# Attention units with partitions in (segment, head pair) order, and the last chunk stored in transfers of 32 rows from two queues

## The chip, the core and the metric

One core of a Trainium2 chip runs the whole program. The metric is the device time of one execution in microseconds; lower is better. Five engines work side by side, each through its own list of instructions in order: TensorE (PE in the profile, its weight loads PEld), VectorE (DVE), ScalarE (ACT), GpSimd (POOL) and SyncE (SP), which only issues transfers. Sixteen DMA engines carry the transfers between HBM and the on-chip memory (SBUF). Matmul results stand in PSUM.

## The reference

`q`, `k`, `v` have shape (8 batches, 8 heads, 576 tokens, 64). For each head two attentions are added, and a two-layer network follows:

```python
q_d, k_d, v_d = (x.reshape(B, H, 144, 4, D).mean(axis=3) for x in (q, k, v))
out_up = np.repeat(sm_attn(q_d, k_d, v_d), 4, axis=2)
mask = np.abs(pos[:, None] - pos[None, :]) < 4
scores = np.where(mask, scale * np.matmul(q, k.transpose(0, 1, 3, 2)), -1e9)
out = out_up + softmax(scores) @ v
x = out.transpose(0, 2, 1, 3).reshape(4608, 512)
h = x @ w_in                                      # 512 -> 2048
y = (np.maximum(h, 0) + alpha * np.minimum(h, 0)) @ w_out   # 2048 -> 512
```

The first attention runs over averages of four tokens; the second sees, for each token, the seven tokens at a distance below four. All inputs and outputs are float32.

## The kernel before

**The network.** The 4608 token rows are cut into 18 chunks of 256 rows (`T`). A chunk takes eight steps (`NP`), so there are 144 steps (`NS`). A step's `hidden` (L752) makes two blocks of 128 hidden columns in 24 matmuls. ACT and DVE apply the slope (L760 to L764), ACT and POOL split the result in a high and a low part `gh` and `gl` (L769, L69), and `product` (L796) adds its 12 matmuls of 128x512 to the chunk's two PSUM tiles `o..._0` and `o..._1`, one for each 128 rows (index `m`). In each step these 12 go through two hidden blocks `j`, three pairs `i` of parts, and `m` innermost, so the two tiles are finished one matmul apart. `finish` (L802, L805) then copies each tile to SBUF on ACT and stores it from SP's queue.

**The order of the output rows.** Batch 0 is computed by matmuls over whole heads (`first_batch`) and its 576 rows are in token order. The seven other batches are computed in 21 *units* on VectorE. A unit (numbers 3 to 23; three to a batch) holds six tokens of each of 32 segments of 18 tokens, for all eight heads. Its 192 rows are kept as six groups (the six tokens) of 32 rows (the segments), so a store of 128 such rows has a DRAM pattern of 4 groups by 32 segments; where the 128 rows cross from one unit to the next, two stores of 2 groups by 32 are issued (function `rows`).

**A unit.** Its SBUF tiles have 128 partitions: 32 segments by 4 head pairs; the two heads of a pair lie side by side in the free dimension (`h2`). Before the change partition p is `32 * pair + segment`. `load_q` (L533) issues two transfers of 128 runs of 1536 B, `load_kv` (L552) two of 128 runs of 3072 B for k and two for v; the DRAM pattern's first dimension is the four pairs, the second the 32 segments. The last unit (23) reads past the end of the tensor, so its second half is cut in three pieces (L545, L547, L549) behind a memset (L544). Scores (`multiply` L591, `total` L595), the maximum and the sums (L604 to L621), and the weighted values (L643 to L653) run on DVE, with a part of the values on POOL (L627). `masks` marks the partitions of the first and the last segment.

**From the unit to the network.** `flip` (L659) transposes the unit's result, so partitions become columns of the PSUM tile `xp`; `join` (L671) adds the first attention's result `od` to it on DVE and writes `xf`, in the order (pair, token, segment); `place` (L685, L69) splits `xf` into the network's operand `xh` and `xl`.

**The first attention of batches 1 to 7** (`down`): six loads `ld` of 72 runs of 2048 B for each head pair (L232), folded on POOL (L72), then a chain of small matmuls, copies and exponentials. POOL's folds stand in the same list as the `gl` (L69) that `product` waits for.

**What sets the order.** Every step of this has a due time in a list of events written in the code; the events are sorted, and the engines get their instructions in that order. Load calls stand there too: q, k and v of unit u + 1 are called during unit u, k after the last read of the old k tile, v after the unit's end, since there is one tile of each kind. All transfers are issued by SP, one after another.

Of the kernel before, what the change touches and what calls it, by code (L numbers as in the profile page):

```python
# [9 lines left out]
F32 = mybir.dt.float32  # L10
# [6 lines left out]
B, H, S, D = 8, 8, 576, 64  # L17
DM, DF = 512, 2048
# [5 lines left out]
HEAD = S * D  # L24
SEG = 18
NF = DF // 128
T = 256
# [6 lines left out]
SB = 2  # L34
# [16 lines left out]
def tile_attention_moe(ctx: ExitStack, tc: tile.TileContext, q, k, v, w_in, w_out, alpha, out):  # L51
    nc = tc.nc
# [3 lines left out]
    two = ctx.enter_context(tc.tile_pool(name="two", bufs=2))  # L56
# [17 lines left out]
    NS = NCHUNK * NF // 2  # L74
    NP = NF // 2
# [5 lines left out]
    masks = {}  # L81

    def build_masks():
        for side, base in (("l", 0), ("r", -31)):
            pat = one.tile([128, 2, 7, 2, 3], F32, tag="lex", name=f"pat_{side}")
            nc.gpsimd.memset(pat, 0.0)
            for half in range(2):
                for dl in range(7):
                    js = [j for j in range(3)
                          if (3 * half + j + dl < 3 if side == "l" else 3 * half + j + dl >= 9)]  # L90
                    if js:
                        nc.gpsimd.memset(pat[:, half, dl, :, js[0]:js[-1] + 1], NEG)
            flag = one.tile([128, 4], F32, tag="flag", name=f"flag_{side}")
            nc.gpsimd.memset(flag, 0.0)
            nc.gpsimd.affine_select(out=flag, in_=flag, pattern=[[-32, 4]], base=base,
                                    channel_multiplier=1, compare_op=ALU.not_equal, fill=1.0)
            fl = one.tile([128, 1], F32, tag="fl", name=f"fl_{side}")
            nc.vector.tensor_reduce(out=fl, in_=flag, axis=AX.X, op=ALU.max)
            m = const.tile([128, 2, 7, 6], F32, name=f"mask_{side}")
            nc.vector.tensor_scalar(m.rearrange("p a b c -> p (a b c)"),  # L100
                                    pat.rearrange("p a b c d -> p (a b c d)"),
                                    fl[:, 0:1], None, op0=ALU.mult)
            masks[side] = m
# [13 lines left out]
    wi, wo = ([[None] * 4, [None] * 4] for _ in range(2))  # L117
# [409 lines left out]
    def unit_base(u):  # L527
        return (u // 3) * H * HEAD + 6 * (u % 3) * D

    def load_q(u):  # L530
        qt = tiles[u, "q"] = late.tile([128, 2, 6, 64], F32, tag="qt", name=f"q{u}")
        for h2 in range(2):
            nc.sync.dma_start(qt[:, h2].rearrange("p t d -> p (t d)"),  # L533
                              bass.AP(q.tensor, unit_base(u) + h2 * HEAD,
                                      [[2 * HEAD, 4], [SEG * D, 32], [1, 384]]))

    def load_kv(u, x):
        src = k if x == "k" else v
        t = tiles[u, x] = late.tile([128, 2, 12, 64], F32, tag=f"{x}t", name=f"{x}{u}")
        for h2 in range(2):  # L540
            off = unit_base(u) + h2 * HEAD - 3 * D
            flat = t[:, h2].rearrange("p t d -> p (t d)")
            if u == 3 * B - 1 and h2 == 1:
                nc.vector.memset(flat[96:128, 576:768], 0.0)  # L544
                nc.sync.dma_start(flat[0:96], bass.AP(src.tensor, off,  # L545
                                                      [[2 * HEAD, 3], [SEG * D, 32], [1, 768]]))
                nc.sync.dma_start(flat[96:127], bass.AP(src.tensor, off + 6 * HEAD,  # L547
                                                        [[SEG * D, 31], [1, 768]]))
                nc.sync.dma_start(flat[127:128, 0:576],  # L549
                                  bass.AP(src.tensor, off + 6 * HEAD + 31 * SEG * D, [[1, 1], [1, 576]]))  # L550
            else:
                nc.sync.dma_start(flat, bass.AP(src.tensor, off,  # L552
                                                [[2 * HEAD, 4], [SEG * D, 32], [1, 768]]))

    def window(t, half, d0, nd):
        tok = 3 * half + d0
# [9 lines left out]
    def local(u, t0, t1):  # L566
        b, jj = u // 3, u % 3
        st = {}
# [92 lines left out]
        def join(i):  # L661
            j0, nt = groups[i]
            odv = od[b].rearrange("p a (s g) -> p a s g", g=9)
            tp = st.pop(("tp", i))
            xf = late.tile([128, 512], F32, tag="xf", name=f"xf{u}_{i}")[:, :128 * nt]
            xf = st["xf", i] = xf.rearrange("p (a t s) -> p a t s", a=4, s=32)
            for par in range(2):
                pos = [(18 * par + 6 * jj + j) // 4 for j in range(j0, j0 + nt)]
                for g in sorted(set(pos)):
                    k0, nk = pos.index(g), pos.count(g)  # L670
                    nc.vector.tensor_tensor(  # L671
                        xf.rearrange("p a t (s e) -> p e t a s", e=2)[:, par, k0:k0 + nk],
                        tp.rearrange("p (t a s e) -> p e t a s", t=4, a=4, e=2)[:, par, k0:k0 + nk],
                        odv[:, :, :, g].unsqueeze(1).to_broadcast([128, nk, 4, 16]), op=ALU.add)

        def place(i, low):
# [11 lines left out]
        def put(i, t):  # L688
            at(t, join, i)
            at(t + 0.05, place, i, False)  # L690
            at(t + 0.3, place, i, True)
# [21 lines left out]
        t = t0  # L713
# [17 lines left out]
        if u + 1 < 3 * B:  # L731
            at((half_done + 0.03) if by_half else t0 + 1.0, load_q, u + 1)
            at(when["total", str((1, 5, 2))] + 0.05, load_kv, u + 1, "k")
            at(t1 + 0.05, load_kv, u + 1, "v")
# [6 lines left out]
    gs, outs, hs = {}, {}, {}  # L741
# [31 lines left out]
    def rows(pos, n):  # L773
        while n:
            if pos < S:
                m = min(n, S - pos)
                ap = bass.AP(out.tensor, pos * DM, [[DM, m], [1, DM]])
            else:
                u, o = divmod(pos, 192)
                m = min(n, 192 - o)  # L780
                row = (u // 3) * S + 6 * (u % 3) + o // 32
                ap = bass.AP(out.tensor, row * DM, [[DM, m // 32], [SEG * DM, 32], [1, DM]])
            yield m, ap
            pos, n = pos + m, n - m

    def product(st):
        c, fp = divmod(st, NP)
        if fp == 0:
            outs[c] = [ps_o.tile([128, DM], F32, tag="po", name=f"o{c}_{m}") for m in range(T // 128)]
        gh, gl = gs.pop(st)  # L790
        for j in range(2):
            f = 2 * fp + j
            n, o = divmod(f, 4)
            for i, (g, w) in enumerate(((gh, 0), (gh, 1), (gl, 0))):
                for m, po in enumerate(outs[c]):
                    nc.tensor.matmul(po, g[:, j, 128 * m:128 * m + 128], wo[w][n][:, o, :],  # L796
                                     start=(f == 0 and i == 0), stop=(f == NF - 1 and i == 2))

    def finish(c):
        for m, po in enumerate(outs.pop(c)):  # L800
            sg = two.tile([128, DM], F32, tag="stage", name=f"sg{c}_{m}", bufs=SB)
            nc.scalar.copy(sg, po)  # L802
            row = 0
            for cnt, ap in rows(T * c + 128 * m, 128):
                nc.sync.dma_start(ap, sg[row:row + cnt, :])  # L805
                row += cnt

    def place_rest():
        hi, lo = (t[:, :, 0:S - 2 * T] for t in operand(2))
        nc.scalar.copy(hi, rest)  # L810
        sub(lo, rest, f32(hi))
# [7 lines left out]
    with tc.tile_pool(name="start", bufs=1) as start:  # L819
        load_pair, load_windows, pair = first_batch(start)  # L820
        todo = [(w, fp) for fp in range(NP) for w in range(2)]
        for step in ORDER.split():
            kind, i = step[0], int(step[1])
# [16 lines left out]
        def at(t, f, *args):  # L840
            events.append((t, len(events), f, args))

        down(1, 0, FIRST[0], 0.0, 0.75, early=True)
    build_masks()
    late = ctx.enter_context(tc.tile_pool(name="late", bufs=1))

    for s in range(NS):
        at(s - 1.95, hidden, s)
        at(s - 1.45, slopes, s)
        at(s - 1.15, larger, s)  # L850
        at(s - 1.0, split, s)
        at(s + 0.6, product, s)
        if s % NP == NP - 1:
            at(s + 1.02, finish, s // NP)

    blocks = [(w, fp, c) for w in range(2) for fp in range(N_EARLY, NP) for c in range(2)]
    at(-1.98, load_raw, 0, N_EARLY)
# [3 lines left out]
    t = T0_DEC  # L861
# [15 lines left out]
    for b in range(2, B):  # L877
        first, end = begin[3 * b - 2], begin[3 * b + 1]
        for hp in range(4):
            down(b, hp, first + (end - first - 0.5) * hp / 4 - (2.7 if b == 2 else 4.5), 0.45)  # L880
    at(3.3, load_q, 3)
    at(3.4, load_kv, 3, "k")
    at(decoded + 0.3, load_kv, 3, "v")
    at(decoded + 0.6, place_rest)
    put = None
    for u in range(3, 3 * B + 1):
# [7 lines left out]
        elif put:  # L894
            at(begin[u] + 0.3, flip, 0)
            put(0, when["before 0"])
            t = when["before 0"] + 0.25 if u == 4 else when["before 1"]
# [31 lines left out]
```

## Time and profile before

| | |
|---|---|
| median of 3 runs | 1025.86 us (1025.6 to 1030.05) |
| the profiled execution, its own time | 1026.39 us |
| its span, first to last instruction | 1024.5 us |
| busy: PE, DVE, ACT, POOL | 960.5, 831.8, 560.4, 487.7 us |
| mean granted TensorE clock | 0.969 |
| moved over DMA | 98.25 MB |

The page cuts the span in 40 slices and gives the busy share of each in tenths. The row DMA is the mean share over 16 DMA engines, so that 2 stands for about four of them at work. In rows of groups the order is: line, engine, operation, output<-inputs, shape, count | busy us, mean ns of one | idle time before and what ended it. Rows of waits give the sum in us, the number of times, and the longest. "SPq" is SP's queue of transfers, and the time of its rows is that of issuing, not of the transfer.

### The profile page before, as it was taken

The page shows a single profiled execution, that of the slowest core. Times are in us where ns is not written, and L with a number is a line of the kernel's source. Part 1 is how long each engine was busy: PE and PEld are TensorE (multiplying, and loading weights), DVE is VectorE, ACT ScalarE, POOL GpSimd, SP SyncE. Part 2 cuts the span into 40 slices and gives each one's busy share as a digit, 9 for nine tenths or more (in the row PEclk, how much of TensorE's full clock was granted, in tenths as well). Part 3 has the DMA queues.
Part 4 walks back from the last instruction along what each step waited for, and adds up shares of the span by engine and source line. Part 5 has one row for each costly group of instructions (what it writes and reads, how often), then busy time and mean ns, then how long its engine had stood idle before and what let it go on. Part 6 is the DMA issues. An engine that isn't in the chain of part 4 may idle for free.

```text
span 1024.5 us, 17852 instructions
## 1 busy us (share of the span) xinstructions
PE 960.5 (94%) x6402; PEld 853.0 (83%) x6402; DVE 831.8 (81%) x1346; ACT 560.4 (55%) x1484; POOL 487.7 (48%) x612
## 2 busy tenths in 40 slices
PE   4877989999999999999999999999999999999995
PEld 4756868898888899988888888888888898989894
DVE  6899978898788899899879888898898899995110
ACT  4767766465555554555555554655555564444442
POOL 2160645676565645555555544655555542333221
PEclk9956989999999999999999999999999999999998
DMA  8947343232322322322322232322322221100000
GB/s 184 228 141 246 111 126 110 96 109 85 115 100 95 106 75 86 109 93 102 107 84 74 92 107 77 116 90 80 104 98 81 93 78 62 73 36 21 1 21 20
DMA packets 59549, 98.25 MB, mean 96 GB/s; under 512 B 19910, under 2 KB 25286, under 8 KB 59462
## 3 DMA queue, kind: packets, MB, share of 16 engines
q1 hardware_dynamic: 59462, 97.12, 30.1%
q8 instruction: 50, 0.82, 0.3%
q14 instruction: 37, 0.30, 0.1%
HBM read 87.67 MB, written 9.44 MB: 95 GB/s over the span
## 4 chain that ended last, share of the span: by engine, by line
PE 74%; DVE 12%; DMA 4%; ACT 3%; issue 2%; SPq 2%; POOL 2%; ACTq 0%; DVEq 0%; POOLq 0%
PE h L752 34%; PE o L796 33%; PE s L263 2%; PE pv L297 2%; DVE temp L193 2%; DMA raw<-in_moe_w_in 1%; PE xp L659 1%; DMA ld<-in_v 1%; PE pT L287 1%; DVE temp L194 1%; DMA k<-in_k 1%; DVE t L764 1%; DVE qk L591 1%; SPq L393 1%; DVE temp L188 1%
## 5 line engine op out<-in xcount | busy, mean ns | idle before, releaser
L69 POOL TENSOR_TENSOR gl<-t,gh 128x512 fp32r<-128x512 f32 x144 | 186.4, 1295 | 312.9 <-ACT gh L769 281.5
L760 ACT ACTIVATE t<-h,slope 128x256 f32<-128x256 f32 x288 | 136.3, 473 | 205.4 <-PE h L752 163.6
L72 POOL TENSOR_TENSOR ld<-ld 72x256 f32<-72x256 f32 x168 | 130.8, 779 | 158.4 <-DMA ld<-in_q 88.6
L752 PE MATMUL h<-xh,wih 128*128 128x256 f32 x1152 | 191.9, 288 | 0.7 <-ACT xh L518 0.7
L764 DVE TENSOR_TENSOR t<-h,t 128x512 f32<-128x512 f32 x144 | 99.0, 687 | 114.8 <-ACT h L761 112.9
L796 PE MATMUL o<-woh,gh 128*128 128x512 f32 x576 | 187.5, 407 | 0.4 <-ACT woh L203 0.4
L752 PE MATMUL h<-xl,wih 128*128 128x256 f32 x1152 | 184.3, 282 | 1.4 <-POOL xl L69 1.4
L752 PE MATMUL h<-xh,wil 128*128 128x256 f32 x1152 | 185.0, 283 | 0.0
L796 PE MATMUL o<-woh,gl 128*128 128x512 f32 x576 | 181.1, 396 | 0.9 <-POOL gl L69 0.9
L796 PE MATMUL o<-wol,gh 128*128 128x512 f32 x576 | 181.4, 396 | 0.2 <-DVE wol L211 0.2
L752 PEld LDWEIGHTS h<-xh,wih 128*128 128x128 f32 x1152 | 164.2, 191 | 10.7 <-issue 1.8
L752 PEld LDWEIGHTS h<-xl,wih 128*128 128x128 f32 x1152 | 157.5, 190 | 1.6 <-POOL xl L69 1.6
L752 PEld LDWEIGHTS h<-xh,wil 128*128 128x128 f32 x1152 | 158.4, 191 | 0.0
L769 ACT CAST gh<-t 128x512 fp32r<-128x512 f32 x144 | 89.1, 619 | 120.7 <-DVE t L764 71.4
L595 DVE TENSOR_REDUCE ls<-qk 128x12 f32<-128x768 f32 (+1 forms) x126 | 136.4, 1082 | 2.8
L796 PEld LDWEIGHTS o<-woh,gl 128*128 128x128 f32 x576 | 108.2, 188 | 27.5 <-POOL gl L69 1.3
L796 PEld LDWEIGHTS o<-wol,gh 128*128 128x128 f32 x576 | 108.1, 188 | 26.8 <-DVE wol L211 1.1
L761 ACT ACTIVATE h<-h,sign 128x256 f32<-128x256 f32 x288 | 126.4, 439 | 0.0
L650 DVE TENSOR_TENSOR lb<-lb,pv 128x384 f32<-128x384 f32 x202 | 113.9, 564 | 5.5
L796 PEld LDWEIGHTS o<-woh,gh 128*128 128x128 f32 x576 | 98.1, 189 | 16.2 <-issue 2.2
L647 DVE TENSOR_TENSOR pv<-v,lb 128x1152 f32<-128x1152 f32 x84 | 93.6, 1115 | 2.6
L591 DVE TENSOR_TENSOR qk<-k,qp 128x768 f32<-128x768 f32 (+1 forms) x78 | 84.1, 1079 | 0.6 <-DMA k<-in_k 0.6
(146 smaller groups left out, 1108.6 us busy)
## 6 DMA issues: line engine op xcount, KB each, us to landing
k<-in_k SPq DMA_DIRECT2D x41, 384.0 KB
v<-in_v SPq DMA_DIRECT2D x41, 384.0 KB
raw<-in_moe_w_in SPq DMA_DIRECT2D x16, 512.0 KB
raw<-in_moe_w_out SPq DMA_DIRECT2D x16, 512.0 KB
ld<-in_q SPq DMA_DIRECT2D x56, 144.0 KB
ld<-in_k SPq DMA_DIRECT2D x56, 144.0 KB
ld<-in_v SPq DMA_DIRECT2D x56, 144.0 KB
q<-in_q SPq DMA_DIRECT2D x42, 192.0 KB
```

The source lines that it names most:

```text
L69: nc.gpsimd.tensor_tensor(o, a, b, op=ALU.subtract)
L72: nc.gpsimd.tensor_tensor(o, a, b, op=ALU.add)
L591: nc.vector.tensor_tensor(st["pr"][:, :nd], window(tiles[u, "k"], half, d0, nd), st["qp", half].unsqueeze(1).to_broadcast([128, nd, 2, 192 ...
L595: nc.vector.tensor_reduce(out=st["s"][:, half, d0:d0 + nd, :].rearrange("p a b -> p (a b)"), in_=st["pr"][:, :nd].rearrange("p a h (t d) - ...
L647: nc.vector.tensor_tensor(st["pr"][:, :nd], window4(tiles[u, "v"], half, d0, nd), prob(half, d0, nd), op=ALU.mult)
L650: nc.vector.tensor_tensor(st["acc"], st["acc"], st["pr"][:, i], op=ALU.add)
L752: nc.tensor.matmul(ph[:, j], w[:, m, 128 * o:128 * o + 128], x[:, m, :], start=(i == 0), stop=(i == 11))
L760: nc.scalar.activation(t[:, j], hs[st][:, j], AF.Copy, scale=slope[:, f:f + 1])
L761: nc.scalar.activation(hs[st][:, j], hs[st][:, j], AF.Copy, scale=sign[:, f:f + 1])
L764: nc.vector.tensor_tensor(gs[st], hs.pop(st), gs[st], op=ALU.max)
L769: nc.scalar.copy(gh, t)
L796: nc.tensor.matmul(po, g[:, j, 128 * m:128 * m + 128], wo[w][n][:, o, :], start=(f == 0 and i == 0), stop=(f == NF - 1 and i == 2))
```

## The change

1. In all unit tiles partition p becomes `4 * segment + pair`. The DRAM patterns of the loads have the 32 segments first and the four pairs second; runs and bytes are the same. The masks' flags move to partitions 0 to 3 and 124 to 127. `join` reads the columns of `xp` in the new order: neighbouring segments of one parity lie 8 columns apart where they lay 2 apart. What it writes is unchanged, and so is everything behind it.
2. The last unit's second half is loaded in four pieces where there were three.
3. In the last of the 144 steps the 12 matmuls of `product` are sorted by `m`.
4. The last chunk has a `finish` of its own: the first tile is copied on ACT, the second on DVE, and each is stored in four transfers of 32 rows, two from SP's queue and two from ACT's.

```diff
-            nc.gpsimd.affine_select(out=flag, in_=flag, pattern=[[-32, 4]], base=base,
+            nc.gpsimd.affine_select(out=flag, in_=flag, pattern=[[-1, 4]], base=base,
...
                               bass.AP(q.tensor, unit_base(u) + h2 * HEAD,
-                                      [[2 * HEAD, 4], [SEG * D, 32], [1, 384]]))
+                                      [[SEG * D, 32], [2 * HEAD, 4], [1, 384]]))
...
             if u == 3 * B - 1 and h2 == 1:
                 nc.vector.memset(flat[96:128, 576:768], 0.0)
-                nc.sync.dma_start(flat[0:96], bass.AP(src.tensor, off,
-                                                      [[2 * HEAD, 3], [SEG * D, 32], [1, 768]]))
-                nc.sync.dma_start(flat[96:127], bass.AP(src.tensor, off + 6 * HEAD,
-                                                        [[SEG * D, 31], [1, 768]]))
+                for s0, n in ((0, 16), (16, 15)):
+                    nc.sync.dma_start(flat[4 * s0:4 * (s0 + n)],
+                                      bass.AP(src.tensor, off + s0 * SEG * D, [[SEG * D, n], [2 * HEAD, 4], [1, 768]]))
+                nc.sync.dma_start(flat[124:127], bass.AP(src.tensor, off + 31 * SEG * D, [[2 * HEAD, 3], [1, 768]]))
...
                 nc.sync.dma_start(flat, bass.AP(src.tensor, off,
-                                                [[2 * HEAD, 4], [SEG * D, 32], [1, 768]]))
+                                                [[SEG * D, 32], [2 * HEAD, 4], [1, 768]]))
...
-                        tp.rearrange("p (t a s e) -> p e t a s", t=4, a=4, e=2)[:, par, k0:k0 + nk],
+                        tp.rearrange("p (t s e a) -> p e t a s", t=4, a=4, e=2)[:, par, k0:k0 + nk],
...
-        for j in range(2):
+        order = [(j, i, m) for j in range(2) for i in range(3) for m in range(T // 128)]
+        if st == NS - 1:
+            order.sort(key=lambda x: x[2])
+        for j, i, m in order:
...
+    def finish_last(c):
+        for m, po in enumerate(outs.pop(c)):
+            sg = two.tile([128, DM], F32, tag="stage", name=f"sg{c}_{m}", bufs=SB)
+            if m == 0:
+                nc.scalar.copy(sg, po)
+            else:
+                nc.vector.tensor_copy(sg, po)
+            for i in range(4):
+                (_, ap), = rows(T * c + 128 * m + 32 * i, 32)
+                (nc.sync if i % 2 == 0 else nc.scalar).dma_start(ap, sg[32 * i:32 * i + 32, :])
...
-            at(s + 1.02, finish, s // NP)
+            at(s + 1.02, finish if s + 1 < NS else finish_last, s // NP)
```

How it moves instructions is seen at three places; everywhere else each engine's list has the same rows in the same order.

PE, the end of the list before: the second half (block j = 1) of the last step's `product`, on the output tiles `o17_0` and `o17_1`.

```order
L796 MATMUL o17_0_11645<-woh3_1529,gh143_11895 128x512
L796 MATMUL o17_1_11646<-woh3_1529,gh143_11895 128x512
L796 MATMUL o17_0_11645<-wol3_1530,gh143_11895 128x512
L796 MATMUL o17_1_11646<-wol3_1530,gh143_11895 128x512
L796 MATMUL o17_0_11645<-woh3_1529,gl143_11896 128x512
L796 MATMUL o17_1_11646<-woh3_1529,gl143_11896 128x512
```

The same end of PE's list in the changed kernel: the last seven matmuls.

```order
L798 MATMUL o17_0_11647<-woh3_1529,gl143_11898 128x512
L798 MATMUL o17_1_11648<-woh3_1529,gh143_11897 128x512
L798 MATMUL o17_1_11648<-wol3_1530,gh143_11897 128x512
L798 MATMUL o17_1_11648<-woh3_1529,gl143_11898 128x512
L798 MATMUL o17_1_11648<-woh3_1529,gh143_11897 128x512
L798 MATMUL o17_1_11648<-wol3_1530,gh143_11897 128x512
L798 MATMUL o17_1_11648<-woh3_1529,gl143_11898 128x512
```

The tile `o17_0` is now complete six matmuls before the end instead of one; the count is the same.

SP's list at its end, before (the shape is groups x rows x columns; x2 stands for two transfers in a row):

```order
L805 DMA out<-sg15_0_11199 4x32x512
L805 DMA out<-sg15_1_11202 2x32x512 x2
L805 DMA out<-sg16_0_11609 4x32x512
L805 DMA out<-sg16_1_11612 4x32x512
L805 DMA out<-sg17_0_11923 2x32x512 x2
L805 DMA out<-sg17_1_11927 4x32x512
```

ACT's list at its end in the changed kernel; SP's ends with the same two rows of L820, and DVE's with a copy of `o17_1` to `sg17_1` (L817):

```order
L760 ACTIVATE t143_11879<-h143_11854,slope_79 128x256
L761 ACTIVATE h143_11854<-h143_11854,sign_78 128x256
L769 CAST gh143_11897<-t143_11879 128x512
L815 COPY sg17_0_11925<-o17_0_11647 128x512
L820 DMA out<-sg17_0_11925 32x512 x2
L820 DMA out<-sg17_1_11931 32x512 x2
```

The three last stores have become eight of one group each, four on each queue; ACT lost the copy of `sg17_1`. The stores of all earlier chunks keep their rows.

SP's list where the last unit's k is loaded, as the difference (- before, + changed):

```order
 L552 DMA k23_10686<-in_k 128x1x768
-L545 DMA k23_10686<-in_k 96x1x768
-L547 DMA k23_10686<-in_k 31x768
+L546 DMA k23_10686<-in_k 64x1x768
+L546 DMA k23_10686<-in_k 60x1x768
+L548 DMA k23_10686<-in_k 3x768
 L549 DMA k23_10686<-in_k 1x576
```

Two pieces became three; the same holds for v. The loads of the other units stand where they stood, with another DRAM pattern.

More of the change, by code (lines that the diff above doesn't have):

```diff
@@ L83, in build_masks @@
     def build_masks():
-        for side, base in (("l", 0), ("r", -31)):
+        for side, base in (("l", 0), ("r", -124)):
             pat = one.tile([128, 2, 7, 2, 3], F32, tag="lex", name=f"pat_{side}")
@@ L790, in product @@
         gh, gl = gs.pop(st)
-        for j in range(2):
+        order = [(j, i, m) for j in range(2) for i in range(3) for m in range(T // 128)]
+        if st == NS - 1:
+            order.sort(key=lambda x: x[2])
+        for j, i, m in order:
             f = 2 * fp + j
             n, o = divmod(f, 4)
[L794 to L797, printed above, removed]
+            g, w = ((gh, 0), (gh, 1), (gl, 0))[i]
+            nc.tensor.matmul(outs[c][m], g[:, j, 128 * m:128 * m + 128], wo[w][n][:, o, :],
+                             start=(f == 0 and i == 0), stop=(f == NF - 1 and i == 2))
     def finish(c):
```

## The prediction

> **What bounds the kernel now.** I read the cores first, then the slices of the page and the chain that ended last, then busy time in stretches.
>
> ```profile
> core 0: 1024.5 us, clock 0.969
> PE   4877989999999999999999999999999999999995
> DMA  8947343232322322322322232322322221100000
> PE 74%; DVE 12%; DMA 4%; ACT 3%; issue 2%; SPq 2%; POOL 2%; ACTq 0%; DVEq 0%; POOLq 0%
> ```
>
> PE is full from the sixth slice to the last but one. The table of stretches gives the stretch, its length, then busy time of PE, PEld, DVE, ACT and POOL with counts, the granted clock, the DMA share and GB/s.
>
> ```profile
> 300.00:500.00 200.00, 199.60 (x1351) 178.83 (x1350) 178.98 (x286) 112.48 (x311) 106.58 (x136) 1.00 0.29 97
> 500.00:700.00 200.00, 193.25 (x1285) 171.90 (x1286) 170.66 (x278) 109.59 (x301) 108.67 (x140) 0.99 0.28 92
> 700.00:900.00 200.00, 199.02 (x1333) 178.39 (x1332) 179.91 (x289) 106.08 (x283) 91.36 (x109) 1.00 0.25 84
> 900.00:1012.40 112.40, 112.40 (x709) 100.58 (x707) 42.26 (x67) 47.90 (x107) 31.37 (x26) 1.00 0.05 16
> 1012.40:1024.50 12.10, 0.01 (x1) 0.00 (x0) 0.00 (x0) 0.89 (x2) 0.00 (x0) 0.59 0.14 43
> ```
>
> Between 300 and 1012.4 PE idles 8.1 us in all (0.4 + 6.75 + 0.98 + 0), so whatever gets faster there has little to give. The 12.1 us behind the last matmul are the largest piece in which no engine computes. The timeline of that end and the DMA row of the stretch 1012 to 1025 (40 slices of 0.325 us) show what fills them:
>
> ```profile
> 1011.78 0.62 PE L796 MATMUL o<-woh,gl 128*128 128x512 f32 x2
> 1012.22 1.07 ACT L802 COPY sg<-o 128x512 f32<-128x512 f32 x2 [4.95 <-PE o L796]
> 1012.83 1.79 SPq L805 DMA_DIRECT2D out<-sg  x3
> DMA  0000001101111331212222122222211111000000
> GB/s 0 0 0 0 0 0 25 19 6 13 32 44 57 63 50 38 69 57 63 69 101 69 50 88 76 82 101 82 88 50 50 50 50 50 19 0 0 0 0 0
> ```
>
> Issuing is over at 1014.62, but bytes flow from 1013.95 to about 1023.4, at 0.1 to 0.2 of the DMA engines. These are 0.5 MB in three stores of 2, 2 and 4 groups of 32 rows. Two stores of chunk 0, whose pattern is 128 rows without groups, behaved otherwise (stretch 161.9 to 166, slices of 0.1025 us; the first number of the L805 row's span is the issue of the first of them):
>
> ```profile
> L805 SPq DMA_DIRECT2D out<-sg x47: 363/582/3653, 162.2 to 1014.1; - x47
> DMA  0000000000069999999999998925746749411134
> GB/s 0 0 0 0 0 0 0 0 0 0 0 260 420 380 340 360 460 360 380 360 400 380 300 240 220 240 40 140 220 180 260 300 155 265 60 30 45 45 60 75
> ```
>
> The same 0.5 MB passed in some 1.7 us (slices 11 to 27) at 300 to 460 GB/s, at 0.9 and more of the engines. The unit loads look like the slow form; here are two v loads, 0.75 MB, in the stretch 151 to 162 (slices of 0.275 us):
>
> ```profile
> DMA  7251565112122222222222222222222222110000
> GB/s 298 97 52 22 201 242 97 56 78 67 56 101 112 89 101 112 101 101 112 101 89 112 101 112 101 101 112 101 101 112 101 101 112 101 67 56 22 0 0 0
> ```
>
> A share of 0.2 to 0.3 for 7 us is four engines of 16. And this is the one piece of 31 rows of the last unit's v (stretch 904 to 914):
>
> ```profile
> GB/s 74 74 74 74 86 74 86 86 49 25 25 25 37 25 25 25 25 25 25 25 25 25 25 25 25 25 25 25 25 25 25 34 0 0 66 0 0 0 0 0
> ```
>
> 25 GB/s is a single engine. So the number of groups in a pattern's first dimension sets how many engines work: 4 groups four (101 GB/s), 31 rows one, 128 rows all. The change puts 32 segments in front in the unit loads and leaves 32 plain rows in the last stores; stores of earlier chunks keep their 2 and 4 groups. [...] No transfer of 32 rows is in this trace.
>
> **The end, step by step.** `o17_1` is still ready at 1011.78 + 0.62 = 1012.40, since the last step keeps its 12 matmuls. `o17_0` is ready five matmuls earlier than before, about 1011.0; its copy and four issues run beside the last six matmuls, and that cover reaches to 1012.4. What ends last is the second tile: copy, second issue on its queue, flight, arrival. The prices:
>
> ```profile
> L764 DVE TENSOR_TENSOR t<-h,t 128x512 f32<-128x512 f32 x144 | 99.0, 687 | 114.8 <-ACT h L761 112.9 <-POOL pv L627 0.8 <-POOL xl L69 0.3
> L802 ACT COPY sg<-o 128x512 f32<-128x512 f32 x36 | 19.2, 585 | 5.0 <-PE o L796 5.0
> L232 SPq DMA_DIRECT2D ld<-in_k x56: 299/300/3312, 41.4 to 812.4; - x56
> ```
>
> - The DVE copy is not in the trace: 0.59 us as ACT's, or 0.69 as DVE's own operation on the same shape from PSUM. I take 0.69, the same engine: 1013.09.
> - One issue ahead on the queue: 0.30 (72 rows, L232) to 0.58 (median of L805). I take 0.30, the nearer in rows: 1013.39.
> - From issue to the first bytes: 0.85 (162.2 to 163.03) or 1.12 (1012.83 to 1013.95). I take 1.0: 1014.39.
> - The bytes: four transfers of 64 KB, half of the pair that took 1.7 us, begun 0.3 earlier: 0.6 left; ends 0.2 and 0.9. 1014.99.
> - From the last bytes to the end of the span: 1.1 to 1.45 before; I take 1.3: 1016.3.
>
> That is 8.2 us less than 1024.5. With all low ends the sum behind 1012.40 is 3.0 us and the gain 9.1; with all high ends it is 4.7 and the gain 7.4. ACT's queue carries no transfer in the trace; its first use may cost nothing or one more delay to the first bytes (1.1), so the low end is 6.3. I count nothing, since its first transfers belong to `o17_0`, which has 1.4 us in hand.
>
> **The loads of the units.** The bytes of a pair of loads take 7 us now; at the 300 to 460 GB/s of the fast stores 0.75 MB would take about 2. The number of issues on SP stays the same but for unit 23. What waits for DMA today:
>
> ```profile
> POOL ld L72 <- DMA ld<-in_v: 62.4, 16, 12.6
> POOL ld L72 <- DMA ld<-in_q: 44.8, 14, 6.9
> DVE qk L591 <- DMA k<-in_k: 0.6, 2, 0.3
> DVE lb L643 <- DMA v<-in_v: 0.6, 1, 0.6
> PE h L752 <- POOL xl L69: 1.4, 1, 1.4
> PE qkT L250 <- POOL gl L69: 1.0, 1, 1.0
> PE o L796 <- POOL gl L69: 0.9, 1, 0.9
> PE pT L287 <- DVE xf L671: 2.6, 2, 1.8
> PE pT L287 <- ACT th L291: 2.1, 2, 1.7
> 599.17 0.73 POOL L72 TENSOR_TENSOR ld<-ld 72x256 f32<-72x256 f32 x1 [10.39 <-DMA ld<-in_v]
> ```
>
> DVE hardly waits for the loads themselves: its own work covers them. POOL waits 107 us for `ld` loads that queue behind unit loads on the same four engines, but POOL is half idle, and stores of earlier chunks (32 rows of 2 KB on an engine, 2.6 us at 25 GB/s) will still stand ahead of some. What reaches PE is the 0.9 us in which `product` waited for a `gl` queued behind the fold at 599.17; I count it whole. Of the other 2.4 us behind POOL and DVE's 1.2 I count 0.6, because other stops (the two rows of pT, 4.7 us, behind DVE and ACT) stand beside them. Sum 1.5. The bounds are 4.5 (1.4 + 1.0 + 0.9 + 1.2) and a loss of 1.4, one more stop of the longest such kind, since every arrival shifts the meeting of five lists.
>
> **Edits at nothing.** Masks are built once, before the units. The last unit's extra pieces are issued on SP near 880 and 900, where PE runs without a gap; if that cover were gone they would cost two issues, 0.6 us. Sorting the last step's matmuls changes no count. `join` has the one price that needs an argument:
>
> ```profile
> L671 DVE TENSOR_TENSOR xf<-xp,od 128x128 f32<-128x128 f32 (+3 forms) x110 | 40.8, 422 | 6.6 <-POOL xl L69 5.4 <-ACT qp L585 0.7 <-PE xp L659 0.5
> L429 ACT COPY qb<-f0T 64x288 f32<-64x288 f32 x16 | 6.3, 392 | 2.7 <-PE f0T L425 2.5
> L291 ACT COPY th<-pT 72x288 f32<-72x288 f32 x56 | 20.2, 398 | 8.0 <-PE pT L287 8.0
> ```
>
> It now reads PSUM at steps of 8 floats instead of 2. Nearest row: L429 reads 288 columns at steps of 72 floats in 392 ns, L291 the same count in a run in 398. So I take 0 for the step; the upper bound is a doubling, 40.8 us of DVE time. [...]
>
> **Sum.** 8.2 + 1.5 = 9.7 us. The profiled execution would take 1026.39 - 9.7 = 1016.7; it stood 0.53 over the median, so the median becomes 1025.86 - 9.7 = **1016.2 us**, with 1012.3 (9.1 + 4.5) and 1021.0 (6.3 - 1.4) as its ends.
>
> **Rivals.**
> - *Only the end gains.* PE's stops move instead of going, as most of them are ended by DVE and ACT and not by POOL: 1025.86 - 8.2 = 1017.7. Chance 0.25.
> - *Small transfers cost a fixed time each, one behind another.* From 1011.6 four per queue at 1.0 + 1.3 us end at 1020.8, then 0.3: the span ends near 1021.1, 3.4 us saved, and 1.5 from the loads: 1021.0. Against it: two stores issued within half a microsecond shared one burst of 1.7 us. [...] Chance 0.05.
> - *Slower: `join` pays for the wider step.* Doubled, it adds 40.8 us to DVE, which is busy 0.9 of 300 to 900; with half of it reaching PE: 1025.86 - 9.7 + 20.4 = 1036.6. It decides from 9.7 / 110 = 0.09 us per `join` that reaches PE. L429 speaks against it; that it is ACT and not DVE leaves it open. Chance 0.05.
> - *Slower: 32 rows are taken like 31.* Then all eight last stores share one engine: 0.5 MB at 25 GB/s is 21 us from 1012.6, plus 1.3: 1034.9, and 1025.86 + 10.4 - 1.5 = 1034.8 if the loads still spread. It decides by the share of DMA at the end. Chance 0.03.
>
> **How the numbers follow.** The forecast has 0.62. Its range and the first rival's lie within 1012.3 to 1021.0 and hold 0.87 together, less a little at the edges, so I give these ends. 0.5%, about what a measurement of this kernel can tell from no change, is 5.1 us, so faster means under 1020.7: 0.62 + 0.25 less 0.01 at the edge is 0.86. Within 0.5%: 0.05 + 0.01 = 0.06. Slower: 0.05 + 0.03 = 0.08.
>
> **What would show it.** At the end: DMA shares of 5 to 9 tenths for under 2 us, the span ending 3.0 to 4.7 us behind the last matmul; more than 6 us there makes the first sum wrong. Unit loads at 0.9 of the engines for 2 to 3 us, and POOL's 107 us of waits for `ld` at most halved. PE's idle time in 300 to 1012 below 8.1 us by 1 or 2. The mean of `join` at 0.42 us; 0.5 or more would show the third rival. The last matmul later than 1012.4 would make the second sum wrong.

## The result, and the profile after

The changed kernel took 1013.83 us (median of 5 runs, 1012.62 to 1017.85), the kernel before 1030.05 (5 runs, 1025.6 to 1035.75, the three of the recorded median among them). The ratio is 0.9855, 95% interval 0.9824 to 0.9885: 12 to 18 us saved. The time lies in the forecast's range (1016.2 us, with 1012.3 to 1021.0); the saving of 9.7 us that the forecast was added up from is below what was measured. The profiled execution took 1012.62 us, its span 1010.8.

The stretches of the changed kernel, cut at its own last matmul (stretch, length, then busy time of PE, PEld, DVE, ACT and POOL with counts, granted clock, DMA share, GB/s):

```profile
300.00:500.00 200.00, 198.34 (x1344) 177.67 (x1343) 177.94 (x284) 111.69 (x310) 110.09 (x142) 1.00 0.31 97
500.00:700.00 200.00, 194.62 (x1315) 173.41 (x1314) 173.50 (x283) 110.47 (x302) 107.72 (x138) 1.00 0.29 90
700.00:900.00 200.00, 199.79 (x1332) 179.02 (x1331) 181.03 (x287) 106.63 (x283) 89.12 (x106) 1.00 0.27 83
900.00:1006.70 106.70, 106.70 (x672) 95.39 (x671) 36.59 (x59) 44.81 (x100) 29.88 (x25) 1.00 0.04 11
1006.70:1010.80 4.10, 0.00 (x0) 0.00 (x0) 0.69 (x1) 0.00 (x0) 0.00 (x0) 0.89 0.51 128
```

The piece behind the last matmul went from 12.1 to 4.1 us. PE's idle time from 300 to the last matmul went from 8.1 to 7.25 us (1.66 + 5.38 + 0.21). The last matmul itself came 5.7 us earlier, at 1006.70.

The end in the timeline of the changed kernel (start, duration, engine, line; a row of a queue holds all its issues):

```profile
1005.33 0.59 ACT L815 COPY sg<-o 128x512 f32<-128x512 f32 x1 [3.78 <-PE o L798]
...
1005.94 2.29 SPq L820 DMA_DIRECT2D out<-sg  x4
1005.95 2.36 ACTq L820 DMA_DIRECT2D out<-sg  x4
...
1006.30 0.40 PE L798 MATMUL o<-woh,gl 128*128 128x512 f32 x1
1006.73 0.69 DVE L817 COPY sg<-o 128x512 f32<-128x512 f32 x1 [5.89 <-PE o L798]
```

The first tile's copy and its four issues lie beside the last matmuls. The second's copy starts 0.03 us after the last matmul. What its bytes do shows in the DMA view from 1005 to 1011, in slices of 0.15 us:

```profile
DMA  0000000000038698998103969999800000000000
GB/s 0 0 0 0 0 0 0 0 0 0 0 68 218 150 246 191 355 301 191 28 0 82 218 164 219 191 355 314 205 0 0 0 0 0 0 0 0 0 0 0
```

There is one burst for each tile, of 0.26 MB in 1.2 to 1.35 us, mostly at 6 to 9 tenths of the engines where before it was 1 to 2 tenths. The unit loads spread in the same way; here is a pair of v loads between 221 and 232 (slices of 0.275 us):

```profile
DMA  0074639669979987531000000854000000005789
GB/s 0 15 186 141 205 78 156 190 257 346 346 268 369 425 335 287 179 82 60 7 0 0 0 0 0 179 156 186 15 0 0 0 0 0 0 0 95 145 279 302
```

The pair issued at 221.0 and 221.6 landed 4.1 and 4.9 us after its issues. In the kernel before, the same pair, issued at 222.7 and 223.4, landed 7.5 and 11.1 us after its issues. POOL's waits for `ld` from `v` and `q` fell from 107.2 to 27.6 us (with those from `k` from 114.5 to 30.9), and `join` costs what it did (422 ns before). These rows are from the waits between 120 and 1008, then from the groups:

```profile
POOL ld L72 <- DMA ld<-in_v: 21.0, 5, 6.3
POOL ld L72 <- DMA ld<-in_q: 6.6, 2, 3.6
POOL ld L72 <- DMA ld<-in_k: 3.3, 1, 3.3
L671 DVE TENSOR_TENSOR xf<-xp,od 128x128 f32<-128x128 f32 (+3 forms) x110 | 40.7, 420 | 6.6 <-POOL xl L69 5.4 <-ACT qp L585 0.7 <-PE xp L659 0.4
```

So the profiled executions differ by 13.7 us: 8.0 at the end, 5.0 between the issue of the first unit load, 123 to 127 us into the span, and the last matmul (888.2 to 883.2), and 0.7 in the start, which the change does not touch and which varies between runs. Of the 5.0, some 1.0 is a stop near 139 us that is 2.7 us long in eight of the fourteen profiles below and 1.7 in the others, with old and new loads alike, and 1.5 a stretch at half clock at 533, which the last section takes up. The 2.4 by which the steps around 252, 262 and 600 got shorter are what PE no longer lost once the loads spread.

### The profile page after: what moved, and what is told of

It reads as the page before. It is cut to its first block, busy times and chain, and to the rows that moved or that the text cites. A ratio compares the mean times of both kernels' runs of the same rounds, so it can differ in the third digit from the quotient of the medians.

```text
span 1010.8 us, 17864 instructions
## 1 busy us (share of the span) xinstructions
PE 960.6 (95%) x6402; PEld 852.7 (84%) x6402; DVE 832.8 (82%) x1347; ACT 560.2 (55%) x1483; POOL 482.1 (48%) x612
## 4 chain that ended last, share of the span: by engine, by line
PE 72%; DVE 15%; ACT 4%; issue 3%; DMA 2%; POOL 2%; SPq 2%; DVEq 0%; ACTq 0%; POOLq 0%
PE o L798 33%; PE h L752 33%; DMA raw<-in_moe_w_out 2%; DVE qk L591 2%; DVE lb L650 2%; PE s L263 2%; DVE t L764 1%; PE pv L297 1%; DVE ls L595 1%; DVE temp L193 1%; DVE pv L647 1%; PE xp L659 1%; PE pT L287 1%; DVE temp L194 1%; DMA ld<-in_q 1%
## 5 line engine op out<-in xcount | busy, mean ns | idle before, releaser
L72 POOL TENSOR_TENSOR ld<-ld 72x256 f32<-72x256 f32 x168 | 125.4, 747 | 73.9 <-DMA ld<-in_q 49.4
```

The lines of the kernel that those rows point to most:

```text
L72: nc.gpsimd.tensor_tensor(o, a, b, op=ALU.add)
```

## The experiments

Theories: (A) the end gains because 32 plain rows spread over all engines; (B) the loads gain for the same reason, by work that waits for them. Rivals: the end gains from the second queue or from smaller transfers alone; the 5 us in the middle are variation between runs. Fourteen profiles are used, one of each kernel named here, of before and of the changed kernel; the middle of a profile is always counted from the issue of the first unit load to the last matmul (the recorded expectations count some 0.4 us less). A time with one run only is not compared finer than 0.5%.

**Each part alone.** The new end without the new order, and the new order without the new end:

```diff
e1: + order.sort(key=lambda x: x[2])        # last step only
    + at(s + 1.02, finish if s + 1 < NS else finish_last, s // NP)
e2: + [[SEG * D, 32], [2 * HEAD, 4], [1, 768]]   # with masks, join and unit 23; old end
```

> Only parts 3 and 4 of the change: the last step's matmuls sorted, the last chunk copied by two engines and stored in eight transfers of 32 rows from two queues; the units as before. If the end is one sum of its own, the time from the last matmul to the end of the span falls from 12.1 to about 4.1 us and the last matmul stays where before has it, up to the variation of a run: 8.0 us less than before (ratio about 0.992). If the two parts of the change lean on each other (stores that still queue behind something of the units), it is less than 7.

Measured: ratio 0.9931 (0.9901 to 0.996), some 7.1 us less; 4.96 us behind the last matmul, as the last transfer landed 2.7 us after its issue and not 1.95. So the same end can differ by 0.9 us from one execution to the next.

> Only parts 1 and 2: segments first in all unit tiles and loads, the old end. Theory A (loads on 16 engines arrive early and PE loses stops behind GpSimd): 1.5 to 3.5 us less than before, the last matmul that much earlier, the stop of 0.87 us near 600 gone, the one of 1.43 near 252 shorter. Theory B (the loads were hidden, and the 5.7 us by which the profiled last matmul moved are variation between runs): within 1 us of before, with the stops of PE behind 125 us unchanged. The 12.1 us after the last matmul stay under both.

Measured: ratio 0.9936 (0.9913 to 0.996), some 6.6 us less (4.1 to 9.0); 12.0 us behind the last matmul. The stop near 600 is gone and the one near 252 is 0.59 us, as theory A has it, but the saving is above A's 1.5 to 3.5 as well as B's 1. The two parts add up to 13.7, within the 12 to 18 of both, so nothing shows that they lean on each other; the intervals would not show a dependence of 2 or 3 us. The order brings several times the 1.5 us forecast.

**Is it the spread, or the new partition order?** The old order of partitions, but each q, k and v load of units 3 to 22 cut in four transfers of 32 segments:

```diff
-                nc.sync.dma_start(flat, ... [[2 * HEAD, 4], [SEG * D, 32], [1, 768]]))
+                for a in range(4):
+                    nc.sync.dma_start(flat[32 * a:32 * a + 32], ... [[SEG * D, 32], [1, 768]]))
```

> The kernel before with its old partition order, but every q, k and v load of units 3 to 22 cut in four transfers of 32 segments, one for each pair. If the number of first-dimension rows alone sets the engines, these too run on 16 engines and the waits of GpSimd for ld loads fall as in the changed order: about the time of the run with the new order alone, less what four times as many issues cost on SyncE (0.3 us each beside other work). If the new order helps in another way (DRAM addresses, join), this stays at the time of before.

Measured: ratio 0.997 (0.995 to 0.999), some 3.1 us less; the last matmul at 1008.53. The spread alone gains, with the old masks and the old `join`. Whether the rest of the 6.6 is the price of four times the issues, the two intervals (1 to 5, 4.1 to 9.0) don't settle.

**Do the stores of earlier chunks matter?** The changed kernel with these in transfers of 32 rows, too:

```diff
-            for cnt, ap in rows(T * c + 128 * m, 128):
+            while row < 128:
...
+                (cnt, ap), = rows(pos, 32 if pos >= S else min(S - pos, 128 - row))
```

> The changed kernel, and the stores of all earlier chunks also cut in transfers of 32 rows (SyncE only), so that no grouped transfer is left but the small pieces of unit 23. If grouped stores still hold up ld loads on their engines and that reaches TensorE: up to 1 us less than the changed kernel. If nothing in the middle waits for transfers any more: the same as the changed kernel within 1 us, about 14 us less than before.

Measured: 1014.49 us, ratio 0.9849 (0.9824 to 0.9873), the same as the changed kernel. POOL's waits for `ld` fall once more, from 30.9 to 4.7 us: the narrow stores did stand ahead of these loads, but that didn't reach PE.

**How much is variation?** The kernel before, twice more:

> The kernel before, unchanged, profiled a second time, to see which part of a run varies by itself. If the 2.5 us by which the changed kernel was ahead at 125 us, where no unit load has been issued yet, and the half clock at 533 us are variation, then the start differs from the first profile by up to 2.5 us, half-clock stretches move, and the stops of 1.4 us near 252 and 0.9 us near 600 stay. If they belong to the kernel, all of it is as in the first profile within 0.5 us.

> The kernel before, unchanged: a third profile of the old loads, to see what of the difference between the kernels is variation from run to run. From the first load of a unit (about 124 us into the span) to the last matmul: 888 us give or take 1.5, as in the two profiles of it and in the one with the new end alone (887.8, 889.4, 889.1). PE stops of 4.4 to 4.8 us in 200 to 300, an end of 12.1 us. Of the 3.4 us stretches at half the granted clock the earlier ones had one to three behind 200 us, near 262, 531 and 685. If these belong to the old loads, this run has at least the two near 531 and 685; if they come by chance, it may have none or one.

Measured: 1026.68 and 1029.32 us. The first unit load is issued at 122.9 and 126.0 us (124.2 in before), so the start does vary. From there to the last matmul it is 889.7 us in both. The second has stops of 4.3 us in 200 to 300, an end of 11.8 us, and stretches at half clock at 533.8 and 687.4, the two that were to show that they belong to the old loads; but before has only the one near 531, and three of the seven profiles with new loads have one near 530 too. The difference in the middle is not variation: four profiles with the old loads lie between 888.2 and 889.7 us, seven with the new between 883.2 and 886.0.

**The end, three ways.** All eight last stores from SP's queue; the last two tiles in two transfers each of 2 groups by 32 rows; and each of the eight transfers cut in 31 rows and one:

```diff
e7: -  (nc.sync if i % 2 == 0 else nc.scalar).dma_start(ap, sg[32 * i:32 * i + 32, :])
    +  nc.sync.dma_start(ap, sg[32 * i:32 * i + 32, :])
e8: -  for i in range(4):
    +  for i in range(2):      # rows(..., 64): 2 groups x 32 rows
...
e9: +  for lo, n in ((0, 31), (31, 1)):
...
```

> The changed kernel with all eight last stores issued from SyncE. Each issue took 0.31 to 0.44 us in the changed kernel, and the last tile's four now stand in one row: the last is issued 1.1 us after the first instead of 0.4, so from the last matmul to the end of the span 4.1 + 0.7 = 4.8 us. If the two queues were needed for bandwidth, it is over 6; if ScalarE's queue only adds delay (its transfers landed 1.95 us after issue, SyncE's 1.6 to 1.8), it is under 4.5.

> The changed kernel, but each of the last two tiles is stored in two transfers of 2 groups of 32 rows, one from each queue; sorting, copies and queues as changed. If the number of engines made the old end long, this end is long again: 32 rows of 2 KB on an engine take 2.6 us, on two engines for each transfer, four transfers, so the last tile's arrive some 5.5 to 6 us after they are issued and the span ends 7 to 8 us behind the last matmul. If instead sorting, the second copying engine and the second queue made the gain, it stays under 5 us.

> The changed kernel with each of the eight last transfers cut in one of 31 rows and one of 1 row: the same rows from the same queues. If a count of 31 falls on a single engine, all 31-row transfers share that engine: about 0.5 MB at 25 GB/s is 21 us from 1006.9, so the span ends about 22 to 24 us behind the last matmul instead of 4.1. If rows spread over engines whatever their count, it ends within 6 us (eight issues on each queue instead of four add 1.6 us).

Measured, behind the last matmul: 5.13, 14.4 and 23.2 us (spans 1014.0, 1023.0 and 1035.5; times 1015.82, 1024.73 and 1037.54). The first two rows are of e8, from 1008 to 1023 in slices of 0.375 us, the third of e9, from 1012 to 1036 in slices of 0.6:

```profile
DMA  0001011111102010111111111111111111100000
GB/s 0 0 16 22 5 16 38 44 38 33 27 38 38 22 44 33 33 55 55 44 55 55 44 55 55 49 49 55 49 49 55 49 49 55 44 22 11 0 0 0
```

```profile
GB/s 10 17 14 10 14 27 24 27 24 27 24 24 27 24 27 24 27 24 27 24 27 24 27 24 27 24 24 27 24 27 24 27 24 27 24 27 17 0 0 0
```

Same bytes, same queues, same copies: some 50 GB/s with 2 groups, 25 with 31 rows. With sorting, both copying engines and both queues kept, e8's end is longer than the 12.1 us of before, and e9's smaller transfers make it longer still; so the spread is the cause. Two queues don't help when the patterns are narrow: e8's four transfers, from both queues, landed 6.5 to 12.7 us after issue, at a DMA share of 0.11 behind the last matmul, as if all shared the same two engines (0.11 of 16 is 1.8). The 7 to 8 us expected had counted two engines for each transfer. With the spread, the second queue looks worth 1.0 us (5.13 against 4.1 in one execution each; e1's 4.96 shows how much such an end varies), and the issues account for it: on one queue the last issue comes at 1011.36, 2.46 us behind the last matmul, and not 1.17; ACT's transfers land 0.2 to 0.3 us later than SP's (1.96 us after issue against 1.61 to 1.78) and give some of that back.

**Both engines on each last tile:**

```diff
-            if m == 0:
-                nc.scalar.copy(sg, po)
-            else:
-                nc.vector.tensor_copy(sg, po)
+            nc.scalar.copy(sg[:, 0:288], po[:, 0:288])
+            nc.vector.tensor_copy(sg[:, 288:], po[:, 288:])
```

> The changed kernel with each of the last two tiles copied by ACT (288 columns) and DVE (224 columns) at once. Theory (the last copy, 0.69 us, is on the path that sets the end): the copy falls to about 0.4 us, and the end from 4.1 to 3.8 us behind the last matmul; the time 0.3 us less than 1013.8, which the timing cannot tell from nothing. Rival (the last copy is covered by the issues of the first tile on the same queues): the end stays at 4.1 us. As a further profile of the new loads: 884.3 us, give or take 1.5, from the first unit load to the last matmul.

Measured: 1015.0 us, ratio 0.9872 (0.9831 to 0.9913), no different from the changed kernel; but 4.65 us behind the last matmul (1007.88), not 3.8. Its timeline:

```profile
1007.37 0.87 ACTq L818 DMA_DIRECT2D out<-sg  x2
1007.48 0.40 PE L798 MATMUL o<-woh,gl 128*128 128x512 f32 x1
1008.33 0.40 ACT L814 COPY sg<-o 128x288 f32<-128x288 f32 x1 [1.42 <-PE o L798]
1008.76 0.39 DVE L815 COPY sg<-o 128x224 f32<-128x224 f32 x1 [1.43 <-ACT sg L814]
1009.19 0.85 ACTq L818 DMA_DIRECT2D out<-sg  x2
```

Two things stood in the way. ACT issued the first tile's stores until 1008.24, so its copy began 0.45 us late; and DVE's half waited for ACT's. The pair ended 1.27 us behind the last matmul (1009.15 - 1007.88) against 0.72 in the changed kernel. This doesn't test the halving, since the halves didn't run together, but it speaks against the rival: a copy that ended 0.55 us later went with an end 0.55 us longer, so the copy is on the path.

**Which load?** The kernel before with only its k loads cut in four, and with only its v loads:

```diff
+                if x == "k":        # e12: "v"
+                    for a in range(4):
+                        nc.sync.dma_start(flat[32 * a:32 * a + 32], ... [[SEG * D, 32], [1, 768]]))
```

> The kernel before with the k loads of units 3 to 22 alone cut in four transfers of 32 segments. Theory (each stop of PE hangs on the fold whose load is queued behind a particular pair of unit loads): the stop near 600 us, whose load follows a k pair, goes; the stops near 252 and 262, whose load follows a v pair, stay, so that 200 to 300 still has 4.4 to 4.8 us of them. Rival (any relief of the queue helps everywhere): 200 to 300 falls to about 3.3 us as well. From the first unit load to the last matmul 886 to 888 us by the theory, 884 to 885 by the rival. The end stays at 12.1 us.

> The kernel before with the v loads of units 3 to 22 alone cut in four transfers of 32 segments. Theory (as for the k loads alone): the stops in 200 to 300 us fall from 4.4 to 4.8 us to between 3.3 and 4.2, and the stop near 600 us, 0.5 to 1.3 us, stays. Rival (what matters is when k is there for DVE): nothing changes in either place. From the first unit load to the last matmul 886 to 888 us by the theory, 888 to 889 by the rival. The end stays at 12.1 us.

Measured: 1023.19 and 1031.27 us, one run each, and these stops of PE:

| profiles | stops in 200 to 300 us | stop near 600 | half-clock windows behind 200 | first unit load to the last matmul |
|---|---|---|---|---|
| old loads (4: before, e5, e6, e1) | 4.3 to 4.8 | 0.48 to 2.06 | 1, 3, 2, 2 | 888.2 to 889.7 |
| v cut (e12) | 4.2 | 1.90 | 3 | 891.5 |
| k cut (e11) | 3.2 | none | 1 | 887.5 |
| q, k and v cut (e3) | 4.2 | none | 1 | 885.7 |
| new order (7) | 3.3 to 3.4 | none | 0, 2, 0, 1, 0, 1, 0 | 883.2 to 886.0 |

(e11 and e12 have one more half-clock window each, at 193 and 195 us. In e11 it costs 1.9 us, and the stop near 137, long here, 1.0; less these two e11 would be at 884.6, as with the new order.) My theory had the stop near 600 behind a k pair and those near 252 and 262 behind a v pair. The first half holds. In the timelines of e6, e11 and the changed kernel, POOL's fold there waits so long for a load queued behind the k loads:

```profile
600.87 0.73 POOL L72 TENSOR_TENSOR ld<-ld 72x256 f32<-72x256 f32 x1 [11.61 <-DMA ld<-in_v]
```

```profile
592.00 0.73 POOL L72 TENSOR_TENSOR ld<-ld 72x256 f32<-72x256 f32 x1 [4.87 <-DMA ld<-in_v]
```

```profile
588.96 0.74 POOL L72 TENSOR_TENSOR ld<-ld 72x256 f32<-72x256 f32 x1 [4.76 <-DMA ld<-in_v]
```

The second half falls: e11, not e12, takes those stops down. What ends the one near 262 are the joins, and ahead of them on DVE stands the first `multiply` of the next unit, which waits for k. The two rows of before, of e6, of e11 and of the changed kernel, from their timelines:

```profile
258.25 1.35 DVE L591 TENSOR_TENSOR qk<-k,qp 128x1152 f32<-128x1152 f32 x1 [0.28 <-DMA k<-in_k]
264.32 0.41 PE L287 MATMUL pT<-ident,dp 96*72 96x96 f32 x3 [1.85 <-DVE xf L671]
```

```profile
258.78 1.36 DVE L591 TENSOR_TENSOR qk<-k,qp 128x1152 f32<-128x1152 f32 x1 [0.91 <-DMA k<-in_k]
264.85 0.41 PE L287 MATMUL pT<-ident,dp 96*72 96x96 f32 x3 [2.47 <-DVE xf L671]
```

```profile
256.70 1.34 DVE L596 TENSOR_TENSOR qk<-k,qp 128x1152 f32<-128x1152 f32 x1
262.76 0.41 PE L287 MATMUL pT<-ident,dp 96*72 96x96 f32 x3 [1.48 <-DVE xf L676]
```

```profile
255.31 1.34 DVE L591 TENSOR_TENSOR qk<-k,qp 128x1152 f32<-128x1152 f32 x1
261.37 0.41 PE L287 MATMUL pT<-ident,dp 96*72 96x96 f32 x3 [1.47 <-DVE xf L671]
```

DVE's wait for k comes back on PE nearly one for one: 0.28 goes with 1.85, 0.91 with 2.47, none with 1.47. So the k loads carry most of the stops near 262 and 600, and cutting v alone takes neither away. The rival for e11 (any relief helps everywhere) had the 3.3 us in 200 to 300 right, but is no better, since e12 relieves the queue as much; what e12 did is what its own rival said (what matters is when k is there).

Two things stay open. The stop near 252 seems to go by another wait, DVE's for v near 234: with old loads 0.57, 0.25, 0.16 us and none stand beside stops of 1.43, 0.91, 1.04 and 0.58; with the new order it is none, and 0.58 to 0.64. And e3, with all three loads cut, doesn't fit: its DVE waits for no k here, and still its stops are 0.94 and 1.83 us. Why e3 keeps 0.8 us that e11 loses is not shown; its q and v loads put more issues on the queue. The rows of e3:

```profile
255.40 1.35 DVE L593 TENSOR_TENSOR qk<-k,qp 128x1152 f32<-128x1152 f32 x1
261.47 0.41 PE L287 MATMUL pT<-ident,dp 96*72 96x96 f32 x3 [1.83 <-DVE xf L673]
```

## Why the prediction was right, and where it was short

- **The spread** held at every place: in the trace of before 4 groups ran at 0.2 to 0.3 of the engines and 31 rows at 0.06 (907 to 911 us), in the changed kernel 32 rows ran mostly at 6 to 9 tenths, and e8 and e9 show the narrow cases at the end itself (0.11 and 0.06). That 32 would be wide, on which the 0.6 us for the last bytes and the 1.5 us for the loads rest, was the author's estimate: no run on record then showed it. What the runs showed in its place are the bursts of 1.2 to 1.35 us and a pair of loads that flows for 3 to 4 us. The fourth rival (32 rows taken like 31) falls with the shares of 6 to 9 tenths.
- **The end**, 8.2 forecast, 8.0 measured. By steps, forecast and then measured: the copy 0.69 and 0.69 with 0.03 ahead of it and 0.03 behind; one issue ahead 0.30 and 0.42 (1007.45 to 1007.87); from the last issue to the last bytes 1.6 and 1.48 (to 1009.35); from there to the end of the span 1.3 and 1.45. That is 3.9 and 4.1. ACT's queue is later than SP's by 0.2 to 0.3 us, not by the 1.1 taken as a bound. Some steps were off by 0.1 to 0.2 both ways and met in the sum.
- **Joins, masks, unit 23**, forecast at nothing: `join` at 420 ns against 422, so the third rival is dead; from 900 on PE has no gap. That PSUM's wider step is free on DVE is shown for this tile only (its 74 joins of 128x128 take 386 ns against 387).
- **The loads**, 1.5 forecast, are the term that was too small: 4.6 us in the profiles (mean of the four with old loads 889.3, of the seven with new ones 884.6), and 6.6 (4.1 to 9.0) by timing. Of the 1.5, the 0.9 behind the fold near 600 was a fair count: that stop is 0.48 to 2.06 us in the four, mean 1.2, and gone in all with the k loads spread. The failing step is "Of the other 2.4 us behind POOL and DVE's 1.2 I count 0.6", with its reason that "DVE hardly waits for the loads themselves: its own work covers them". The stops in 200 to 300 fell by 1.2 us, since the little that DVE waited for k and v stood ahead of what PE waits for; I had taken the stops that DVE ends as independent of the loads. And one kind of cost I didn't price at all, the half-clock windows below: 2.0 a run with old loads, 0.6 with new, at about 1.5 us, makes 2.1. Together 1.2 + 1.2 + 2.1 = 4.5 of the 4.6. That the 2.1 belong to the loads is not shown: with four and seven profiles the difference can be chance.
- **The first rival** (only the end gains, 1017.7) falls with e2: the order alone is worth at least 4 us. **Small transfers one behind another** falls with the two bursts of 1.2 to 1.35 us; e7 shows what is left of it, 0.46 us an issue on one queue. Here eight transfers of 64 KB took 4.1 us behind the last matmul where three of 128 and 256 KB took 12.1, and e8's four of 128 KB, on few engines again, 14.4: the number of engines decided.
- **The signs.** POOL's waits were to be "at most halved" and fell to a quarter, 107.2 to 27.6; what is left is mostly the narrow stores ahead of the `ld` loads, as I had expected (4.7 in e4). PE's idle time behind 300 fell by 0.9 us where 1 or 2 were named. The pair of unit loads shown flows for 3 to 4 us, not 2 to 3, at 3 to 9 tenths of the engines.
- **The base, and some luck.** The sum starts from 1025.86, the median of the three runs given. The longer series of before have medians of 1028.3, 1028.4 and 1030.05 (21, 11 and 5 runs). From 1030.05 the same sum would have given some 1020.4 us, with 1016.5 to 1025.2, and the 1013.83 measured lies below that. A base that was low and a saving that was too small cancel in part, so the time came out nearer to the forecast than the saving did: 9.7 us forecast, 12 to 18 measured.

## What to carry to other kernels

Read the DMA share of a transfer as a number of engines: here shares of 0.06, 0.11 and 0.2 to 0.3 went with 31 rows, 2 groups and 4 groups in a pattern's first dimension, and a reordering of partitions or a cut into plain pieces of 32 rows mended that without a byte less. Then price what waits: a short wait on a loaded engine, placed ahead of what the busiest engine needs, can come back whole, as the 0.3 to 0.9 us near 258 did, however small it looks in the list of waits. Check a forecast's saving against the measured saving, and not only time against time. At a kernel's end, give the last copy to an engine that isn't issuing stores: in e10 ACT's began 0.45 us late behind its own issues.

## What the runs showed of the hardware

**Short stops, and a window at half clock behind some.** In these runs a stop of PE of 1.4 us can be followed by one window of 3.4 us at half the granted clock (0.51 in e5), which costs about 1.5 us (the same 20 steps, 617.4 to 745.7 in before, take 128.3 to 128.5 us in the ten profiles without such a window near 685 and 129.8 to 129.9 in the four with one). The same stop, ended by the same operation, in e5 and in the changed kernel; in these stretches the first number is PE's busy time and the third from the end the clock:

```profile
681.90:685.30 3.40, 1.99 (x18) 1.42 (x15) 2.94 (x12) 3.21 (x11) 0.21 (x1) 1.00 0.38 113
685.30:688.70 3.40, 3.40 (x10) 2.62 (x9) 3.23 (x6) 0.61 (x2) 0.00 (x0) 0.51 0.45 145
688.70:692.10 3.40, 3.40 (x29) 3.36 (x29) 1.41 (x2) 0.40 (x2) 2.94 (x4) 0.99 0.27 100
```

```profile
675.40:678.80 3.40, 2.90 (x27) 2.33 (x25) 3.13 (x8) 2.25 (x6) 1.94 (x2) 1.00 0.30 55
678.80:682.20 3.40, 2.50 (x14) 2.08 (x15) 3.14 (x9) 2.13 (x8) 0.00 (x0) 1.00 0.47 162
682.20:685.60 3.40, 3.40 (x28) 3.27 (x27) 3.26 (x5) 0.62 (x1) 2.29 (x3) 1.00 0.50 167
```

In the clock records of before and of the changed kernel, twelve in each trace, the changes lie whole multiples of 3.4133 us apart, to about 1 ns; a cell is one step of this grid. In e5 the stop of 1.41 us falls inside one cell, and the next is slow; in the changed kernel 1.40 us is split over two, and no cell is. Lying inside one cell is not enough, though: at 0.15 and 0.20 of the way through, below, it did so too. Counted over the fourteen profiles, the stop near 680 was followed by a slow window in the four where it began 0.23 to 0.57 of the way through a cell, and in none of the ten where it began at 0.15, 0.20 or 0.64 to 0.93. The stop of 2.4 to 2.5 us near 528, which every kernel here has, was followed by one in ten, beginning at 0.84 to 1.00 or up to 0.45, and not in the four that began at 0.46 to 0.56. So the place of a stop seems to decide whether it costs 1.4 or 2.9 us, and that place moves from run to run: 0.15, 0.24 and 0.51 in the three profiles of before, whose stops near 600 are 0.87, 0.48 and 2.06 us long. That the place in the cell is the cause is read from these rows; no run moved a stop on purpose, and it stays open whether the new loads would keep their few slow windows under another start.

**Two queues, the same engines.** Four transfers of 2 groups from two queues ran at about 50 GB/s in all (e8), twice the 25 GB/s of e9; their DMA shares behind the last matmul, 0.11 and 0.06, are about two engines of 16 and one. The second queue brought no further engines here.
